# Attention with a cached K and V: K and V requests interleaved, K paced by the transposes, V requested one unit later

## The chip, the cores and the metric

One core of one Trainium2 chip. The metric is the time of one execution in microseconds on the device. All executions that are compared here are of the fast state; two of the repeated executions (404.68 us at a mean clock of 0.992, 400.10 us at 0.996) fell in the slow state and are left out of the ratios. A ratio is the mean time of one kernel's fast runs over the mean of the other kernel's fast runs of the same rounds, so it is not quite the ratio of the medians that are quoted beside it.

## The reference

```python
B, Sq, D = 8, 112, 640
H, Sk, Dh = 32, 512, 192
q = (x @ wq).reshape(B, Sq, H, Dh).transpose(0, 2, 1, 3)
scores = jnp.einsum("bhqd,bhkd->bhqk", q, k_cache) * (Dh ** -0.5)
p = softmax(scores, axis=-1)
o = jnp.einsum("bhqk,bhkd->bhqd", p, v_cache)
return o.transpose(0, 2, 1, 3).reshape(B, Sq, H * Dh) @ wo      # all bf16
```

K and V are 50 MB each and are read once. They are most of the 118.7 MB that the kernel moves.

## The kernel before

The work is cut into 64 units: 8 groups of 4 heads, and 8 batches in each group. K and V of a unit are 0.79 MB each and are requested in four pieces of 192 KB. One engine, SyncE, issues all requests in one list, in order. Each request first waits for its own semaphore values, and while it waits, everything behind it in the list waits too. In the profile of this kernel the list stood so for 39.0 us on K transposes and 29.5 us on PV matmuls.

```python
NK, NV, NT = 3, 4, 3                     # buffers of raw K, of V, of transposed K
...
def load_k(u):
    ...
    for h in range(KP[u]):               # KP[u] is 4
        add(kr[u % NK]..., src[:, cs], mK[u % NK], ...,
            [(vKT, 4 * (u - NK + 1))])   # all four transposes of unit u-3 have ended

def load_v(u):
    for a in range(4):
        add(vs[u % NV]..., v_cache[b, 4 * g + a]..., mV[u % NV], ...,
            [(pPV, u - NV + 1)])         # the PV matmuls of unit u-4 have ended
...
for u in range(4, NU + 1):
    if u < NU:
        load_k(u)
    if u - 1 >= 3:
        load_v(u - 1)
    ...                                  # then this unit's wq or wo pieces, if any
```

What hangs on V and K on the other engines:

```python
# GpSimd: copy three quarters of V into another layout, then (in its own order) reorder wq pieces
def middle(u):
    W(gp, mV[u % NV], 64 * (u // NV + 1))            # all four V pieces of the unit have landed
    W(gp, pPV, u - NM + 1)
    gp.tensor_copy(vm[u % NM]..., vs[u % NV]...).then_inc(gM, 1)

# ScalarE: the last of four exponentials of a unit
def exp(u, a):
    W(act, pS, 4 * u + a + 1)
    if a == 3 and u >= 2:
        W(act, gM, u + 1)                            # the V copy of this unit is done
    ...

# TensorE: scores of a unit
def do_S(u):
    ...
    W(pe, aEX, 4 * u)                                # all exponentials of the unit before
    ...

# TensorE: the first projection of group g waits for all reordered wq pieces
if k == "Q" and c == 0:
    W(pe, gW, DC * g)
```

So a late V reaches TensorE by two ways: V copy, fourth exponential, scores of the next unit; or V copy, wq reordering behind it, first projection of the next group. VectorE transposes K (four instructions for a unit, `do_KT`), and these wait for all four K pieces of the unit.

## Time and profile before

| | before |
|---|---|
| median of the first 3 runs | 392.25 us (391.72 to 393.08) |
| span of the profiled execution | 390.9 us |
| TensorE busy | 385.9 us, 99% |
| DMA engines | 91.6% of the span |
| TensorE idle in the middle of the run | about 1.3 us |

The views are shown in the prediction. In a timeline the columns are start and duration in us, engine, line of the program, operation, output and input tile and the number of merged instructions. What stands in brackets is the engine's idle time just before, and what ended it. A line of the waits view is: waiter, released by; total us, number of times, longest.

### The profile page before, as it was taken

The page shows a single profiled execution, that of the slowest core. Times are in us where ns is not written, and L with a number is a line of the kernel's source. Part 1 is how long each engine was busy: PE and PEld are TensorE (multiplying, and loading weights), DVE is VectorE, ACT ScalarE, POOL GpSimd, SP SyncE. Part 2 cuts the span into 40 slices and gives each one's busy share as a digit, 9 for nine tenths or more (in the row PEclk, how much of TensorE's full clock was granted, in tenths as well). Part 3 has the DMA queues.
Part 4 walks back from the last instruction along what each step waited for, and adds up shares of the span by engine and source line. Part 5 has one row for each costly group of instructions (what it writes and reads, how often), then busy time and mean ns, then how long its engine had stood idle before and what let it go on. Part 6 is the DMA issues. An engine that isn't in the chain of part 4 may idle for free.

```text
span 390.9 us, 19834 instructions
## 1 busy us (share of the span) xinstructions
PE 385.9 (99%) x8865; PEld 243.1 (62%) x8262; DVE 283.3 (72%) x506; ACT 250.3 (64%) x550; POOL 152.7 (39%) x352
## 2 busy tenths in 40 slices
PE   8999989999999999999999999999999999999997
PEld 3555766666666666666665666665666665667764
DVE  1665688687786777776787776876778776789935
ACT  2867765766656765657746667557665667657662
POOL 5442453344343354234352354332553332333331
PEclk9999999999999999999999999999999999999999
DMA  8999999999999999899999999989998789989912
GB/s 266 375 371 373 348 315 368 341 344 366 317 357 338 299 323 351 283 282 313 338 314 319 299 286 350 337 287 294 312 346 289 247 279 296 339 289 303 312 45 70
DMA packets 88585, 120.00 MB, mean 307 GB/s; under 512 B 9777, under 2 KB 88497, under 8 KB 88497
## 3 DMA queue, kind: packets, MB, share of 16 engines
q1 hardware_dynamic: 88496, 118.72, 91.6%
q8 instruction: 68, 1.11, 1.2%
q14 instruction: 21, 0.16, 0.1%
HBM read 117.54 MB, written 1.15 MB: 304 GB/s over the span
## 4 chain that ended last, share of the span: by engine, by line
PE 98%; DMA 1%; DVE 0%; ACT 0%; issue 0%
PE ps L967 22%; PE ps L858 22%; PE ps L928 22%; PE ps L949 21%; PE ps L978 6%; PE ps L887 2%; DMA xs<-in_x_dram 1%; PE ps L854 1%; PE ps L872 1%; PE ps L892 0%; DVE kt L1106 0%; DVE acc L1126 0%; ACT oT L1064 0%; ACT pT L1047 0%; DVE xs L1129 0%
## 5 line engine op out<-in xcount | busy, mean ns | idle before, releaser
L1106 DVE STREAM_TRANSPOSE kt<-kr 128x384 int32<-128x384 int32 x256 | 195.0, 869 | 8.1 <-DMA kr<-in_k_cache_dram 8.1
L1047 ACT ACTIVATE pT<-ps 128x448 bf16<-128x448 f32 x256 | 130.7, 562 | 82.4 <-PE ps L949 82.4
L949 PEld LDWEIGHTS ps<-qT,kt 32*128 32x128 bf16 x6144 | 77.0, 93 | 29.6 <-issue 19.1
L928 PE MATMUL ps<-wos,oT 128*128 128x320 bf16 (+2 forms) x342 | 92.9, 298 | 0.0
L967 PE MATMUL ps<-vm,pT 128*128 128x193 bf16 x768 | 91.5, 247 | 1.1 <-ACT oT L1064 0.8
L858 PE MATMUL ps<-wos,oT 128*128 128x320 bf16 (+1 forms) x340 | 91.3, 296 | 0.0
L1226 POOL TENSOR_SCALAR bad<-rinv 112x4 f32<-112x4 f32 x64 | 14.6, 228 | 195.9 <-DVE rinv L1112 195.9
L949 PE MATMUL ps<-qT,kt 32*128 32x112 bf16 x6144 | 87.3, 208 | 0.4 <-DVE kt L1106 0.3
L967 PEld LDWEIGHTS ps<-vm,pT 128*128 128x128 bf16 x768 | 67.8, 97 | 22.1 <-ACT oT L1064 11.6
L1209 POOL COPY vm<-vs 128x1152 int32<-128x1152 int32 x64 | 73.4, 1147 | 16.9 <-issue 9.5
L858 PE MATMUL ps<-xT,wqs 128*128 128x448 bf16 (+2 forms) x226 | 74.1, 341 | 0.0
L928 PE MATMUL ps<-xT,wqs 128*128 128x448 bf16 (+1 forms) x210 | 73.5, 350 | 0.0
L1054 ACT ACTIVATE os<-ps,rinv 112x192 bf16<-112x192 f32 x128 | 47.9, 436 | 28.5 <-DVE rinv L1112 28.5
L967 PE MATMUL ps<-vs,pT 128*128 128x193 bf16 x256 | 62.6, 245 | 0.0
L928 PEld LDWEIGHTS ps<-wos,oT 128*128 128x128 bf16 x342 | 33.2, 97 | 43.0 <-issue 35.9
L1031 ACT ACTIVATE qT<-ps 128x448 bf16<-128x448 f32 x96 | 47.8, 554 | 18.5 <-PE ps L928 12.6
L1129 DVE TENSOR_TENSOR acc<-ps,acc 128x320 f32<-128x320 f32 x84 | 37.4, 486 | 26.3 <-PE ps L928 26.0
L1064 ACT ACTIVATE oT<-ps 128x672 bf16<-128x672 bf16 x64 | 46.5, 726 | 2.1 <-PE ps L978 2.1
L1112 DVE RECIPROCAL rinv<-ps 112x4 f32<-112x4 f32 x64 | 11.1, 174 | 49.6 <-PE ps L967 49.6
L928 PEld LDWEIGHTS ps<-xT,wqs 128*128 128x128 bf16 x210 | 20.4, 97 | 34.2 <-issue 29.2
L1115 DVE TENSOR_TENSOR os<-ps,rinv 112x384 bf16<-112x384 f32 x64 | 35.7, 558 | 7.3 <-DVE rinv L1112 0.5
L1202 POOL COPY wqs<-wqr 128x384 bf16<-128x384 bf16 x70 | 33.2, 506 | 5.3 <-DMA wqr<-in_wq_dram 5.3
(44 smaller groups left out, 156.3 us busy)
## 6 DMA issues: line engine op xcount, KB each, us to landing
kr<-in_k_cache_dram SPq DMA_DIRECT2D x256, 192.0 KB, 4.2
vs<-in_v_cache_dram SPq DMA_DIRECT2D x256, 192.0 KB, 4.0
wos<-in_wo_dram SPq DMA_DIRECT2D x48, 160.0 KB, 4.2
wqr<-in_wq_dram SPq DMA_DIRECT2D x35, 192.0 KB, 5.3
wqs<-in_wq_dram SPq DMA_DIRECT2D x5, 192.0 KB, 4.3
out_dram<-xs SPq DMA_DIRECT2D x6, 160.0 KB, 1.8
xs<-in_x_dram SPq DMA_DIRECT2D x2, 320.0 KB, 3.4
xs<-in_x_dram SPq DMA_DIRECT2D x1, 480.0 KB, 5.5
```

Of the source, the lines that this page charges most:

```text
L858: return pe.add_instruction(mybir.InstMatmult(name=nc.get_next_instruction_name(), engine=mybir.EngineType.PE, ins=[pe.lower_ap_or_imm(rhs ...
L928: mm = (pe.matmul if h == hs[0] and f == 0 else held)(ps[:, bank_of(pair, h), cs], w, rhs[h][:, cs], q == 0, q == n - 1 and f == cuts - 1)
L949: mm = pe.matmul(ps[:, a, SQ * t:SQ * (t + 1)], kt[u % NT][p, t, c // 2, :, c % 2], qT[g % 2][p, c, SQ * b:SQ * (b + 1)], start=(c == 0), ...
L967: mm = pe.matmul(pv[:, k, e, 0:DH + 1], pT[u % 2][:, a, t, :], src[:, a, v0:v0 + DH + 1], start=(t == 0), stop=(t == 3), skip_group_check= ...
L1031: act.activation(qT[g % 2][:, c, HQ * h:HQ * (h + 1)], ps[:, bank_of_Q0(n) if g == 0 else 6 + h, 0:HQ], ACTF.Copy).then_inc(aQ, 1)
L1047: act.activation(pT[u % 2][:, a, :, 0:SQ], ps[:, a, 0:4 * SQ].rearrange("p (t q) -> p t q", t=4), ACTF.Exp, scale=scale).then_inc(aEX, 1)
L1054: ins = act.activation(os_[u % 2][:, DH * (2 + e):DH * (3 + e)], pv_of(u)[0:SQ, 1, e, 0:DH], ACTF.Copy, scale=rinv[:, u % 4, 2 + e:3 + e])
L1064: act.activation(oT[:, :, SQ * b:SQ * (b + 1)].rearrange("p (k c) q -> p k c q", k=2), src.rearrange("p k (c q) -> p k c q", c=3), ACTF.Co ...
L1106: dve.transpose(dst, src).then_inc(vKT, 1)
L1115: dve.tensor_tensor(os_[u % 2][:, 0:2 * DH].rearrange("p (e d) -> p e d", e=2), pv[0:SQ, 0, :, 0:DH], rinv[:, u % 4, 0:2][:, :, None].broa ...
L1129: ins = dve.tensor_tensor(ob[:, m, cs] if g == NG - 1 else acc[:, m, cs], src, acc[:, m, cs], op=ALU.add)
L1209: gp.tensor_copy(vm[u % NM][:].rearrange("p a (t w) -> p a t w", w=RW)[:, :, :, 0:DH].bitcast(I32), vs[u % NV][:, :, 32:32 + 3 * DH].rearr ...
```

## The change

The intent is to even out the requests. K and V pieces of a unit alternate, each K piece is held until one more transpose has ended, so that requests follow the pace of the consumer, and V is requested with the K of the unit two later in place of one later. One weight piece may go between the second and third pair, another after the fourth.

```diff
-            def load_k(u):
+            def load_k(u, parts=range(4)):
...
-                for h in range(KP[u]):
+                for h in parts:
...
-                        [(vKT, 4 * (u - NK + 1))])
+                        [(vKT, 4 * (u - NK + 1) + (h if u >= 4 else 0))])
-            def load_v(u):
+            def load_v(u, parts=range(4)):
...
-            for u in range(4, NU + 1):
-                if u < NU:
-                    load_k(u)
-                if u - 1 >= 3:
-                    load_v(u - 1)
+            for u in range(4, NU + 2):
+                w = []
...                                       (this unit's wq and wo pieces are put into w)
+                for h in range(4):
+                    if u < NU:
+                        load_k(u, [h])
+                    if u - 2 >= 3:
+                        load_v(u - 2, [h])
+                    if h % 2 and w:
+                        w.pop(0)()
```

More of the change, by code (lines that the diff above doesn't have):

```diff
@@ L1260, in load_wo @@
                         [(pO, 2 * MT * (g - 1))])
-            def load_k(u):
+            def load_k(u, parts=range(4)):
                 g, b = divmod(u, B)
                 src = k_cache[b, 4 * g:4 * g + 4].rearrange("a (j s) d -> (a j) (s d)", s=16)
-                for h in range(KP[u]):
+                for h in parts:
                     cs = slice(16 // KP[u] * DH * h, 16 // KP[u] * DH * (h + 1))
                     add(kr[u % NK][:].rearrange("p s d -> p (s d)")[:, cs], src[:, cs], mK[u % NK], 16 * sum(KP[u % NK:u + 1:NK]),
-                        [(vKT, 4 * (u - NK + 1))])
-            def load_v(u):
+                        [(vKT, 4 * (u - NK + 1) + (h if u >= 4 else 0))])
+            def load_v(u, parts=range(4)):
                 g, b = divmod(u, B)
-                for a in range(4):
+                for a in parts:
                     add(vs[u % NV][:, a, 32:32 + 4 * DH], v_cache[b, 4 * g + a].rearrange("(m t) d -> m (t d)", t=4),
@@ L1298, in on_sync @@
                     if 0 <= d < DC:
-                        load_wq(g, d)
+                        w.append(lambda g=g, d=d: load_wq(g, d))
                 for g in range(1, NG):
@@ L1302, in on_sync @@
                     if 0 <= d < 3:
-                        load_wo(g, d)
+                        w.append(lambda g=g, d=d: load_wo(g, d))
+                for h in range(4):
[5 more added lines that the diff above has]
+                        w.pop(0)()
+                assert not w
             for n, (dst, src, s, count, waits) in enumerate(loads):
```

## The prediction

> **What bounds the kernel now.** I read the page first, then the chain that ended last, then TensorE's own waits, then stretches of time, and only then the timelines of GpSimd, SyncE, ScalarE and TensorE around the places where the DMA queue is full. The page gives the busy times, the DMA row and the chain by engine:
>
> ```profile
> PE 385.9 (99%) x8865; PEld 243.1 (62%) x8262; DVE 283.3 (72%) x506; ACT 250.3 (64%) x550; POOL 152.7 (39%) x352
> ...
> DMA  8999999999999999899999999989998789989912
> ...
> q1 hardware_dynamic: 88496, 118.72, 91.6%
> ...
> PE 98%; DMA 1%; DVE 0%; ACT 0%; issue 0%
> ```
>
> The reader is to see two things near their limit: TensorE has work for 385.9 of 390.9 us, and the DMA engines are taken 91.6% of the time, yet only TensorE is on the chain that sets the end. TensorE's waits are short (columns: waiter, its line, released by; total us, times, longest):
>
> ```profile
> PE ps L984 <- DVE wt L1096: 1.0, 1, 1.0
> PE ps L967 <- ACT oT L1064: 0.8, 1, 0.8
> PE ps L854 <- DMA xs<-in_x_dram: 0.4, 1, 0.4
> PE ps L949 <- DVE kt L1106: 0.3, 1, 0.3
> ```
>
> In the middle of the run TensorE loses only 0.8 + 0.3 us and some 0.2 us more; the rest of its 5.0 us idle lies before the first x piece (some 1.3) and at the end, after all loads (some 2.3). So a perfect supply of K and V can give back about 1.3 us of 392.25, or 0.3%. A loss has no such ceiling: any wait newly put before TensorE stays in the time, since there is almost no slack to recover it.
>
> Where can such a wait come from? The stretches (busy us of PE, PEld, DVE, ACT, POOL; clock; DMA share; GB/s) show where DMA is really short:
>
> ```profile
> 20.00:30.00 10.00, 10.00 (x245) 5.64 (x231) 6.67 (x10) 6.77 (x15) 4.13 (x7) 1.00 1.07 371
> 60.00:70.00 10.00, 10.00 (x257) 6.04 (x238) 8.00 (x14) 5.66 (x13) 4.28 (x10) 1.00 1.06 363
> 200.00:300.00 100.00, 100.00 (x2341) 62.79 (x2158) 75.32 (x134) 63.83 (x143) 40.47 (x90) 1.00 0.97 315
> ```
>
> Up to about 100 us the queue is working off the start-up loads at 350 to 375 GB/s; afterwards demand is near 315. In the first stage V is consumed as soon as it lands. GpSimd's timeline at unit 8 (start, duration, what; in brackets its idle time before), the landing of that unit's V, and the requests on SyncE:
>
> ```profile
> 63.05 1.14 POOL L1209 COPY vm<-vs 128x1152 int32<-128x1152 int32 x1 [2.46 <-issue]
> 64.13 0.95 POOL L1202 COPY wqs<-wqr 128x384 bf16<-128x384 bf16 x2
> ```
>
> ```profile
> L1309 SPq DMA_DIRECT2D vs<-in_v_cache_dram x4: 430/433/439, 56.0 to 57.4; - x4
> ...
> DMA to landing us min/median/max: 4.1/4.3/5.5
> ```
>
> ```profile
> 55.96 1.87 SPq L1309 DMA_DIRECT2D vs<-in_v_cache_dram  x4
> 57.87 0.91 SPq L1309 DMA_DIRECT2D wos<-in_wo_dram  x2
> 58.83 2.30 SPq L1309 DMA_DIRECT2D kr<-in_k_cache_dram  x4
> ```
>
> The last V piece of unit 8 is requested at 57.4 and takes up to 5.5 us: 62.9. GpSimd, idle for 2.46 us, starts its copy of V at 63.05. So what the profile calls "issue" here is a wait for V. The same sum fits units 3 (28.8 + 6.3 = 35.1, copy at 35.28), 4 (34.2 + 5.7, copy at 39.97), 6, 9 and 10: the copy is bound by V's landing from unit 3 to about unit 10. Behind it in GpSimd's order stands the reordering of the last wq piece of the next group, 64.13 to 65.08, and the first projection of that group needs it:
>
> ```profile
> 65.62 0.35 PE L928 MATMUL ps<-xT,wqs 128*128 128x448 bf16 x1
> ```
>
> Slack 0.54 us. This is the thinnest place in the kernel.
>
> [...] So one held K piece holds every request after it, V too. The trace agrees in form: SyncE's waits, 39.0 us for K transposes and 29.5 for PV matmuls, stand between requests. [...] one unit's 96 score matmuls take 1.36 us with DMA at 373 GB/s (at 33 us) and at 84 GB/s (at 372 us). So a smoother DMA does not make matmuls faster. [...] Here no wait exceeds 1.0 us and the clock is 1.000 throughout[...].
>
> **The change part by part.** No bytes, requests, transposes or matmuls are added or removed: 256 K and 256 V requests of 192 KB stay. Three things change.
>
> (a) The hold. Pieces 1 to 3 of K wait for one, two, three more transposes of 0.87 us. The buffer is free already, so this is pacing. In the first stage SyncE arrives late anyway. Unit 9's third hold needs 31 transposes, done at 51.12 + 2.29 = 53.4 us, while its K was requested at 54.06. Cost there about nil. In the later stage the piece goes 3 to 5 us later; six transposes separate the third hold from the first use of that K. I read leads of 7 to 10 us from VectorE's timeline (for example 217.2 to 226.5), against 0.5 us to issue and 4 to 5.5 to land. The thinnest are units 14 and 16 at 5.0 us (81.85 to 86.85), where VectorE may wait some 0.5 us. TensorE has transposes in hand there. Cost 0.
>
> (b) Alternation. SyncE needs 0.46 us for each request, so 9 per unit already take 4.2 of some 5.9 us. The order among them changes, the rate hardly does. Cost 0.
>
> (c) V one unit later. This is the part with a price. V of unit v is complete after the K of unit v+2 instead of before it, and behind one more weight piece. While the queue is backlogged, I count positions. For unit 8 the new end is the old end of unit 10's K, 58.83 + 2.30 = 61.13, plus one wq request, 0.46: 61.6 instead of 57.83, so 3.8 us later. For units 3, 4 and 9 the same count gives 3.9; for 6 and 7 about 5; for 5 about 3.2. (By bytes at 370 GB/s: 0.79 MB of K and 0.39 MB of weights are 3.2 us.)
>
> What takes it up? The fourth exponential of a unit waits for the V copy, the next unit's scores for that exponential. From the copy's end to the exponential, and from its end to the scores, ScalarE's and TensorE's timelines give together 2.1 us for unit 3 (36.43 to 37.25, 37.8 to 39.10), 2.9 for 4, 3.7 for 5, 3.1 for 6, 3.5 for 7, 2.6 for 9, 3.6 for 10. For unit 8 the wq reordering leaves 0.54. Delay less slack: 1.8, 1.0, 0, 2, 1.5, 3.3, 1.3, 0. These do not add up: each microsecond that TensorE has lost gives the next V another microsecond. The largest counts, 3.3 at unit 8. I take off 0.5 because a tail of K waits and queue pressure moves out of the way: 2.8 us in all. After 100 us the copy starts well over 9 us after V's request and nothing is lost. Gains: at most part of the 1.3 us; the 0.8 there is ScalarE's behind a transpose, not DMA's, so none. Sum: 392.25 + 2.8 = 395.0 us.
>
> **The rivals.** First, the smooth supply is neutral: SyncE catches up sooner in the first stage since K stands less in front of waits, V lands only about 2 us later, and the slack takes nearly all of it. For it: the overlap of landing times and the DMA share under 1 at 50 to 60 us. Against it: V is on the edge in six units. It would give 392 to 393. Second, the hold takes the place of the removed burst: VectorE's transposes wait for K in the later stage, and with the in-order queue this feeds back on V. For it: the 5.0 us leads at units 14 and 16. Against it: other leads are 7 us and more, and VectorE is 72% busy. Should it come regularly, 0.2 us in each of 50 units make 402. Third, [...] a few us of half-rate matmuls, 397 to 399. Fourth, a gain over 2%, 7.8 us: there are not that many idle microseconds on TensorE.
>
> **Range and chances.** The mechanism puts it between 1 and 5 us above; the first rival reaches down to 392, the third up to 398 or so. Predicted 395.0, 8 in 10 within 392.2 and 398.2. Faster by over 2%: 0.01. Within 2%: 0.92. Slower by over 2% (above 400.1): 0.07, from the second and third rivals.
>
> **What would show it.** Right: GpSimd's V copies for units 3 to 10 start 3 to 4 us later; TensorE gets waits between 37 and 70 us, the largest for GpSimd's wq reordering, some 3 us, none longer after 100 us; matmul durations and bytes unchanged; K transposes wait under 2 us in all after 80 us. The V hold by position is wrong if V lands less than 2 us later at unit 8. The whole is wrong if TensorE's idle time falls, if its waits are spread over all units, or if score matmuls change their 1.36 us.

That matmuls can run at half rate was measured only afterwards (granted clock 0.50 from 66 to 68 us in the profile of the change). That a held K piece holds V too was also measured afterwards (4.1 us, in hold and V later). For the first stage the profile before has 375 GB/s from 10 to 20 us, 371 to 373 in the 20 us after and 315 to 363 from 40 to 100 us.

## The result, and the profile after

| | before | changed |
|---|---|---|
| median of 6 runs | 392.69 us (391.72 to 393.61) | 399.05 us (397.08 to 400.25) |
| ratio of fast runs | 1 | 1.0159 (95%: 1.0127 to 1.0191) |
| span of the profiled execution | 390.9 us | 396.2 us |

The change makes the kernel slower by 1.6%, or 6.2 us. The prediction had 2.8 us, and its range ended at 398.2. The same fields of the changed kernel's page:

```profile
PE 388.1 (98%) x8865; PEld 244.0 (62%) x8262; DVE 284.0 (72%) x506; ACT 251.5 (63%) x550; POOL 153.3 (39%) x352
...
PEclk9999998999999999999999999999999999999999
DMA  8999999789999999999999989998998979999922
...
q1 hardware_dynamic: 88496, 118.72, 90.5%
...
PE 86%; DMA 4%; issue 4%; SPq 3%; DVE 2%; POOL 1%; ACT 0%; DVEq 0%; ACTq 0%
```

The same bytes and packets are moved. TensorE is busy 2.2 us longer for the same 8865 matmuls, and one slice of the clock row shows an 8. DMA has a hole in the eighth slice, where SyncE now waits for K transposes (6.2 us between 69 and 80 us). The chain that ended last is no longer all TensorE: DMA, SyncE and GpSimd are on it. TensorE's waits:

```profile
PE ps L949 <- ACT pT L1047: 3.2, 3, 2.0
PE ps L984 <- DVE wt L1096: 1.0, 1, 1.0
PE ps L967 <- ACT oT L1064: 0.8, 1, 0.8
PE ps L854 <- DMA xs<-in_x_dram: 0.2, 1, 0.2
```

The first line is new: the scores (L949) wait three times for ScalarE's exponentials. The largest is 2.0 us, before unit 8. It can be followed back through four engines. First SyncE, the last V piece of unit 7, in the kernel before (one burst of four) and in the changed kernel:

```profile
49.99 1.86 SPq L1309 DMA_DIRECT2D vs<-in_v_cache_dram  x4
```

```profile
57.01 0.43 SPq L1314 DMA_DIRECT2D vs<-in_v_cache_dram  x1
```

Then GpSimd's copy of that V, ScalarE's fourth exponential of unit 7 and TensorE's scores of unit 8, first before:

```profile
56.27 1.14 POOL L1209 COPY vm<-vs 128x1152 int32<-128x1152 int32 x1
...
57.78 1.43 ACT L1047 ACTIVATE pT<-ps 128x448 bf16<-128x448 f32 x3
...
61.04 1.36 PE L949 MATMUL ps<-qT,kt 32*128 32x112 bf16 x96
62.33 0.47 PE L978 MATMUL ps<-ident,os 112*128 112x112 bf16 x6
```

and in the changed kernel:

```profile
62.08 1.15 POOL L1209 COPY vm<-vs 128x1152 int32<-128x1152 int32 x1 [4.80 <-issue]
...
63.32 0.54 ACT L1047 ACTIVATE pT<-ps 128x448 bf16<-128x448 f32 x1 [3.64 <-POOL vm L1209]
...
64.01 1.81 PE L949 MATMUL ps<-qT,kt 32*128 32x112 bf16 x96 [1.99 <-ACT pT L1047]
65.75 0.74 PE L978 MATMUL ps<-ident,os 112*128 112x112 bf16 x6
```

The V request ends at 57.44 instead of 51.85, the copy starts 5.8 us later, the exponential waits 3.64 us for it, and TensorE stands for 1.99 us. Then comes something else. The 96 score matmuls take 1.81 us instead of 1.36 and the six transposes 0.74 instead of 0.47: TensorE's clock has dropped, after this wait of 1.99 us and one of 0.83 us some 5 us earlier, and the next stretch of ten microseconds shows it (the last three columns are clock, DMA share, GB/s):

```profile
60.00:70.00 10.00, 8.01 (x145) 4.84 (x131) 4.91 (x10) 3.75 (x8) 4.75 (x9) 0.83 1.03 356
70.00:80.00 10.00, 10.00 (x256) 5.96 (x238) 7.75 (x15) 5.93 (x13) 3.22 (x8) 1.00 0.73 226
```

In steps of 2 us the clock is 0.69 from 64 us, 0.50 from 66, 0.96 from 68 and 1.00 from 70. From the scores of unit 8 to the projection after them TensorE needs 4.58 us before (61.04 to 65.62) and 6.18 us now (64.01 to 70.19): the slow clock costs 1.6 us in this execution. Of the 6 executions 4 had a mean clock of 0.996, and 2 had 1.000.

Where the time goes, unit by unit, I read from VectorE's reciprocal, which starts right after each unit's PV matmuls: its start in one kernel less its start in the kernel before. For the changed kernel the lateness grows by 0.9 us at unit 3, 3.7 at units 7 and 8, 0.4 over units 9 to 17 and 0.3 over the 46 units after (0.1 us came at units 4 to 6). It is mainly the start of the run that is hurt, as predicted; the size is not as predicted.

### The profile page after: what moved, and what is told of

Same layout as the page of the kernel before. It is cut to its first block, busy times and chain, and to the rows that moved or that the text cites. A ratio compares the mean times of both kernels' runs of the same rounds, so it can differ in the third digit from the quotient of the medians.

```text
span 396.2 us, 19834 instructions
## 1 busy us (share of the span) xinstructions
PE 388.1 (98%) x8865; PEld 244.0 (62%) x8262; DVE 284.0 (72%) x506; ACT 251.5 (63%) x550; POOL 153.3 (39%) x352
## 4 chain that ended last, share of the span: by engine, by line
PE 86%; DMA 4%; issue 4%; SPq 3%; DVE 2%; POOL 1%; ACT 0%; DVEq 0%; ACTq 0%
PE ps L967 20%; PE ps L858 19%; PE ps L928 19%; PE ps L949 19%; PE ps L978 6%; DMA kr<-in_k_cache_dram 3%; SPq L1314 3%; PE ps L887 2%; DVE kt L1106 1%; PE ps L854 1%; DMA xs<-in_x_dram 1%; PE ps L872 1%; POOL vm L1209 1%; ACT pT L1047 0%; PE ps L892 0%
## 5 line engine op out<-in xcount | busy, mean ns | idle before, releaser
L1106 DVE STREAM_TRANSPOSE kt<-kr 128x384 int32<-128x384 int32 x256 | 196.1, 872 | 12.4 <-DMA kr<-in_k_cache_dram 12.4
L949 PEld LDWEIGHTS ps<-qT,kt 32*128 32x128 bf16 x6144 | 77.5, 93 | 32.8 <-issue 19.0
L949 PE MATMUL ps<-qT,kt 32*128 32x112 bf16 x6144 | 87.7, 209 | 3.5 <-ACT pT L1047 3.2
```

The lines of the kernel that those rows point to most:

```text
L949: mm = pe.matmul(ps[:, a, SQ * t:SQ * (t + 1)], kt[u % NT][p, t, c // 2, :, c % 2], qT[g % 2][p, c, SQ * b:SQ * (b + 1)], start=(c == 0), ...
L1106: dve.transpose(dst, src).then_inc(vKT, 1)
```

## The experiments

All were run with 5 rounds and all gave correct results. The median of the kernel before was between 392.71 and 393.31 us in each call, so 0.1% is 0.4 us. The four calls ran on four different chips, so kernels of one call compare more safely than kernels of two. In the rows with alternation a weight piece goes out after the second and the fourth pair, as in the change; only the row "weights last" puts them behind all V pieces.

| kernel | hold | alternation | V later | ratio to before (95%) | median us |
|---|---|---|---|---|---|
| changed, again | yes | yes | yes | 1.0167 (1.0142 to 1.0193) | 399.14 |
| V later only | | | yes | 1.0077 (1.0058 to 1.0097) | 395.45 |
| V later only, again | | | yes | 1.0051 (1.0028 to 1.0073) | 395.36 |
| hold only | yes | | | 1.0006 (0.9985 to 1.0027) | 393.21 |
| alternation only | | yes | | 1.0215 (1.0191 to 1.0238) | 401.45 |
| alternation and hold | yes | yes | | 1.0232 (1.0201 to 1.0263) | 402.82 |
| alternation and V later | | yes | yes | 1.0120 (1.0098 to 1.0143) | 397.56 |
| the same, weights last | | yes | yes | 1.0081 (1.0060 to 1.0101) | 396.22 |
| hold and V later | yes | | yes | 1.0121 (1.0088 to 1.0153) | 397.10 |

**First call: the parts one by one.** My theory A was the prediction's: V later is what costs, in the start-up backlog, with the clock added. The rival B was the hold.

The changed kernel again, for a second profile:

> The changed kernel once more, for its spread and a second profile. Theory A (V one unit later starves the V copy in the first 70 us, TensorE stands before the scores of unit 8, and its clock drops there): 397 to 400 us, 4 to 5 us of the loss by unit 8, a stretch of lowered clock between 60 and 70 us in most executions. Theory B (the hold on K pieces is what costs): the same time, so this run tells nothing between them.

399.14 us, and in its profile the clock stayed at 1.000: a span of 395.2 us with 3.9 us of waits before scores. Two of these three waits are in the first stage, the third comes after it:

```profile
100.40 1.36 PE L949 MATMUL ps<-qT,kt 32*128 32x112 bf16 x96 [1.06 <-ACT pT L1047]
```

Five of its 6 executions were fast, two of them at 0.996. Over both measurements the 5 fast executions at 1.000 have a mean of 398.0 us and the 6 at 0.996 one of 399.6 us.

V one unit later only, K in bursts without a hold:

```diff
                 if u < NU:
                     load_k(u)
-                if u - 1 >= 3:
-                    load_v(u - 1)
+                if u - 2 >= 3 and u - 2 < NU:
+                    load_v(u - 2)
```

> K pieces in bursts without a hold, only V requested one unit later. Theory A: nearly the whole loss, 396 to 400 us, with V copies of units 3 to 8 some 4 to 6 us later than before. Theory B (hold): near 393 us.

395.45 us, 0.8% or 3.0 us. That is close to the prediction's own figure for this part, 2.8 us, and half of the change's loss. A second measurement, in the fourth call, gave 2.0 us, a third of it. The waits of TensorE show both ways by which V was to reach it, the exponential and, at the predicted place, the wq reordering:

```profile
PE ps L949 <- ACT pT L1047: 1.6, 2, 1.0
PE ps L984 <- DVE wt L1096: 1.0, 1, 1.0
PE ps L928 <- POOL wqs L1202: 0.9, 1, 0.9
```

Theory A said nearly the whole loss; it got half.

The hold only, in the order of the kernel before:

```diff
-                        [(vKT, 4 * (u - NK + 1))])
+                        [(vKT, 4 * (u - NK + 1) + (h if u >= 4 else 0))])
```

> The order and bursts of the kernel before, each K piece held for one more transpose. Theory A: 392 to 393.5 us, since the queue arrives later than the hold in the first stage. Theory B: 396 us or more, with VectorE waiting for K.

393.21 us, no difference. Rival B falls in its plain form: the hold alone costs nothing in the mean. Its profiled execution shows something else. TensorE had two short waits around the scores of unit 7, and after them its clock was lowered from about 58 to 62 us (mean clock of this execution 0.996), which shows in the PV matmuls (0.56 us for three):

```profile
56.41 0.57 PE L949 MATMUL ps<-qT,kt 32*128 32x112 bf16 x31 [0.96 <-issue]
58.21 0.56 PE L967 MATMUL ps<-vm,pT 128*128 128x193 bf16 x3 [0.82 <-ACT oT L1064]
```

At the same place in the kernel before, with the second wait only, they take 0.43 us:

```profile
57.95 0.43 PE L967 MATMUL ps<-vm,pT 128*128 128x193 bf16 x3 [0.85 <-ACT oT L1064]
```

Alternation only, with V where it was and no hold:

```diff
+                for h in range(4):
+                    if u < NU:
+                        load_k(u, [h])
+                    if u - 1 >= 3 and u - 1 < NU:
+                        load_v(u - 1, [h])
+                    if h % 2 and w:
+                        w.pop(0)()
```

> K and V pieces alternately, V of the unit before as in the kernel before, no hold. Theory A: 392 to 393.5 us. A third theory, that the interleaving itself slows the landing of both, since the last of four pieces comes later: V copies 1 to 2 us later at units 3 to 8, 393.5 to 395 us. Theory B: as before.

401.45 us, worse than the whole change. None of the three theories had this. V is in time now (unit 7 copied at 57.61, before 56.27, of which 1.2 us are a later start of this execution), and up to unit 9 the kernel loses nothing. But VectorE waits for K all through the run; in the kernel before this was 8.1 us in 4 times:

```profile
DVE kt L1106 <- DMA kr<-in_k_cache_dram: 52.1, 37, 3.7
```

SyncE's timeline in the later stage shows why:

```profile
210.49 0.44 SPq L1314 DMA_DIRECT2D kr<-in_k_cache_dram  x1
212.69 0.33 SPq L1314 DMA_DIRECT2D vs<-in_v_cache_dram  x1
213.06 0.43 SPq L1314 DMA_DIRECT2D kr<-in_k_cache_dram  x1
```

After the first K piece of a unit the next in the list is a V piece that must wait for a PV (210.93 to 212.69). The other three K pieces stand behind it, although their buffer is free. In the kernel before all four K pieces were out before that wait.

**Second call: pairs, and the stage.** Theory C, formed on the first call: once V is late, the hold on a K piece also delays the V piece behind it. Theory D: V later is what makes alternation bearable.

Alternation and V later, without the hold (the changed kernel's loop, the hold's term taken out):

> K and V pieces alternately and V one unit later, no hold; with the hold missing from the change. If the hold costs nothing once V is late (theory A, as in the prediction): as the changed kernel, near 399 us. If the hold on a K piece delays the V piece behind it in the same queue after about 65 us (theory C, formed on the first four runs): 396 to 397.5 us, with V copies of units 10 to 16 some 2 us earlier than in the changed kernel.

397.56 us, 1.2%. It is as theory C has it, between V later alone and the whole change. Its interval still overlaps a little with those of the changed kernel. Its V copies of units 10 to 16 start 1.5 to 3.5 us earlier than in the changed kernel, of which 1.3 to 2.2 us are because this execution as a whole is ahead there.

Hold and V later, in bursts:

> K pieces in bursts, held, and V one unit later. Theory A: as V later alone, 395.5 us. Theory C: 396.5 to 398.5 us, the loss by unit 9 as with V later alone (2.5 to 3 us) and some 1 us more between units 10 and 16.

397.10 us, 1.2%, again as theory C. SyncE's timeline shows the hold at work. The K pieces of unit 14 and the V pieces of unit 12 behind them, first in V later alone, then with the hold:

```profile
80.22 1.85 SPq L1309 DMA_DIRECT2D kr<-in_k_cache_dram  x4
82.12 1.85 SPq L1309 DMA_DIRECT2D vs<-in_v_cache_dram  x4
```

```profile
81.76 4.41 SPq L1309 DMA_DIRECT2D kr<-in_k_cache_dram  x4
86.22 1.86 SPq L1309 DMA_DIRECT2D vs<-in_v_cache_dram  x4
```

The four K requests take 4.41 us in place of 1.85, and V goes out 4.1 us later; only 0.6 us of this is a later state of the whole execution. The profiles of all kernels with V later separate cleanly after the first stage. Lateness gained over units 9 to 17, by the reciprocals: with the hold 0.4 and 1.1 us (changed, two profiles) and 0.4 (this one); without it -0.4 in this call's alternating kernel and -0.4 in V later alone. Two later profiles with the hold gave 0.9 and 1.0, two without it -0.4 each. So five profiles with the hold lie 0.8 to 1.5 us above four without. (The -0.4 is the zero line: the hold alone gives it too, so it is the one profile of the kernel before that lost 0.4 us there.) ScalarE waited for a V copy 9 or 10 times in the changed kernel and this one, 5 to 7 times in the two without.

Alternation and hold, V in its old place:

> Alternately and held, V of the unit before (not later). The run with alternation alone showed VectorE waiting 52 us for K, since K pieces stand behind V pieces that wait for a PV. Theory D: that is a crossing of two waits in one queue, the hold makes it no better, 400 to 406 us, and V one unit later is what makes alternation bearable. If the hold evens it out instead: 393 to 397 us.

402.82 us, and VectorE waits 51.2 us for K: theory D. The hold does not help alternation; V later does, by taking the PV wait out of K's way. With alternation it saves 3.7 us (1.0215 to 1.0120), with alternation and hold 2.7 (1.0232 to the 1.0163 of the changed kernel's two measurements), even though it costs 2 to 3 us by itself.

The whole change from unit 24 on only, the old order before:

```diff
+                late = u >= 24
...                                       (late: the changed loop; else: the loop of before)
+                        [(vKT, 4 * (u - NK + 1) + (h if u >= 24 else 0))])
```

> The order of the kernel before up to unit 23, the whole change from unit 24 on. All theories that put the loss into the start-up backlog (A, C): 392 to 393.5 us. If the change costs a little in every unit: 395 us or more.

393.08 us, ratio 1.0009 (0.9989 to 1.0030). The change costs nothing where the queue has no backlog, and gains nothing there either.

**Third call: the wait itself, and the queue position.** Here the kernel before was made to wait at unit 8 with all its loads as they were:

```diff
                 W(pe, aEX, 4 * u)
+                if u == 8:
+                    W(pe, vKT, 38)        # 39 in the second kernel
```

> The kernel before; TensorE alone is held before the scores of unit 8 until two more K transposes have ended, so that it stands there some 2.3 us, with all loads as before. If a wait costs only its own length: +2.3 us, 395 us. If the clock drops after it as in the profile of the changed kernel (some 4 us at a lower rate): +3.5 to +4.5 us, 396.5 to 397 us, in some or all executions, with a mean clock of 0.996 in those.

396.57 us, ratio 1.0072 (1.0037 to 1.0108). The executions fall into two kinds: 394.55 and 394.98 us at a mean clock of 1.000, and four from 396.49 to 398.02 at 0.996. In the profiled one the wait grew to 4.2 us, because K came late for that transpose, so the length of the wait is less well known than I had wanted.

> The same with one more transpose, a wait of some 3.1 us. Own length only: +3.1 us, 395.8 us. With the clock's drop: +4.5 to +6 us, 397.5 to 399 us. [...]

397.61 us, ratio 1.0104 (1.0074 to 1.0134). The wait was 3.07 us as set:

```profile
63.50 2.43 PE L951 MATMUL ps<-qT,kt 32*128 32x112 bf16 x96 [3.07 <-DVE kt L1108]
65.86 0.74 PE L980 MATMUL ps<-ident,os 112*128 112x112 bf16 x6
```

One execution kept 1.000 and took 396.1 us; the five others had 0.991 or 0.996 and took 397.36 to 398.25. From the scores to the next projection it is 7.47 us (63.50 to 70.97) in place of 4.58: the slow clock cost 2.9 us there, almost as much as the wait.

The changed kernel with the three wo loads of group 1 three units later:

```diff
-                    d = u - (8 * g - 1)
+                    d = u - (8 * g - 1) - (3 if g == 1 else 0)
```

> The changed kernel, but the three wo loads of group 1 requested with units 10 to 12 in place of 7 to 9. If the V of unit 7 is late because of what stands before it in the queue: its copy 1.5 to 2 us earlier than in the changed kernel, the wait before the scores of unit 8 under 1 us, the clock stays up, 396 to 397.5 us; units 10 to 13 may lose up to 1 us more. If the position in the queue is not it: 399 us.

397.08 us, ratio 1.0105 (1.0073 to 1.0137), about 2.3 us less than the changed kernel. The total is as expected, the way only in part: V of unit 7 was copied at 61.40, just 0.7 us earlier than in the changed kernel. TensorE's waits moved to units 3 and 7 (it gained 1.8 us of lateness at unit 3 and 0.8 over units 4 to 6) and only 0.4 us came at units 7 and 8, without a drop of the clock in the profiled execution. One profile can't say how much is position and how much is the clock.

The kernel before with V ahead of K up to unit 13:

```diff
+                if u < 14:
+                    load_v(u - 1)
                 if u < NU:
                     load_k(u)
-                if u - 1 >= 3:
+                if u >= 14:
                     load_v(u - 1)
```

> The kernel before with V ahead of K in each unit up to 13. V copies of units 3 to 10 some 2 us earlier. Since no wait of TensorE in the kernel before comes from V: 392 to 393.5 us, the same. If V on the edge costs the kernel before something that its one profile does not show: up to 1 us less. If K then comes late: 394 us or more.

393.68 us, ratio 1.0019 (0.9981 to 1.0057): the same. V copies at units 3 and 8 came 2.2 and 1.7 us earlier, at unit 9 1.3 us, at units 4 to 7 only 0.4 to 1.2 us, and from unit 10 on not at all. V on the edge costs the kernel before nothing that this could take away.

**Fourth call: what was still open.** V later alone had explained half. Left were the clock, and what alternation and hold add.

The changed kernel with TensorE kept at work before unit 8, by matmuls of zeros into a bank that the scores then overwrite:

```diff
+                if u == 8:
+                    W(pe, aEX, 4 * u - 3)
+                    for j in range(36):   # 56 in the next kernel
+                        (held if j else pe.matmul)(ps[:, 0, 0:112], wt[:], wt[:, 0:112], True, True)
                 W(pe, aEX, 4 * u)
```

> The changed kernel, with 36 matmuls of zeros (some 1.7 us at the full clock) before the wait for the scores of unit 8, into a bank that is then overwritten. If the lowered clock after that wait is part of the loss (theory E): no or shorter stretches of lowered clock near unit 8, and 0.5 to 2 us less than the changed kernel in the mean, 397 to 398.5 us. If the drop costs nothing of note or stays: 399 us or more.

The 1.7 us of this expectation is an estimate that the profile before bears out: its projection matmuls of 320 columns start 0.136 us apart, so 112 columns are 0.048 us, 36 of them 1.7 us and 56 of them 2.7.

398.89 us, ratio 1.0156 (1.0128 to 1.0184), so not clearly less than the changed kernel. The clock was 1.000 in 5 of 6 executions, as intended, but the work of zeros takes 1.9 us whether or not there is a wait to fill, and executions at 1.000 still ranged from 396.95 to 400.11. This is inconclusive on the size. The changed kernel's loss is not mainly the clock: its own executions at 1.000 have a mean of 398.0 us, some 5 us above the kernel before.

> The kernel before with the wait of some 3.1 us before the scores of unit 8, filled with 56 matmuls of zeros (some 2.7 us). Theory E: only the wait's own length is left, +3 us, 396 us, clock 1.000. Otherwise as without the filling, 397.6 us.

396.50 us, ratio 1.0088 (1.0068 to 1.0108). All six executions had 1.000, and the scores after the filled wait take their usual time:

```profile
64.57 1.36 PE L955 MATMUL ps<-qT,kt 32*128 32x112 bf16 x96 [0.35 <-DVE kt L1112]
```

Beside 2.43 us and one execution of six at 1.000 in the unfilled twin, this shows that here the idleness before the scores brings the drop. What that is worth in the mean is less clear: 1.1 us by the medians, 0.6 by the ratios, and the intervals overlap.

Alternation and V later, no hold (its term taken out as before), with weight pieces after V:

```diff
-                    if h % 2 and w:
-                        w.pop(0)()
-                assert not w
+                for f in w:
+                    f()
```

> Alternately and V one unit later, no hold, but each unit's weight pieces after its V pieces as in the kernel before. If the weight piece ahead of the last V pieces is what alternation adds over V later alone: 395.5 to 396.3 us, last V requests of units 4 to 9 as with V later alone. If it is the alternation of K and V itself: near 397.5 us.

396.22 us, ratio 1.0081 (1.0060 to 1.0101), against 1.0120 (1.0098 to 1.0143) with the weight piece in front of the last two V pieces. The last V requests of units 4 to 9 go out 0 to 1.8 us earlier than with the weight piece in front and within 2 us of those of the first profile of V later alone, so the expectation holds roughly. The weight piece is thus probably most of what alternation added to V later, some 1.5 us; but the two were measured in different calls, and their intervals just touch. The profiled execution here was a late one, 398.45 us, and it shows the predicted wait of the first projection for the wq reordering at full size:

```profile
PE ps L928 <- POOL wqs L1202: 2.2, 1, 2.2
```

V later alone, again:

> V one unit later alone, again, beside the alternating kernel on the same chip: 395.5 us, +0.8%. If it comes out near 397 us, the difference between it and the kernels with alternation or hold added was one of chip and call, and only the whole change against V later alone is clear.

395.36 us, ratio 1.0051 (1.0028 to 1.0073). Its profiled execution, the slowest of the fast ones, waits 3.9 us before scores, 2.04 of it before unit 8, and only 0.3 us for the wq reordering. The scores after that wait of 2.04 us took their 1.36 us, and the mean clock of this execution was 1.000: a wait of this length was not always followed by a lowered clock. Its interval and that of the alternating kernel with weights last overlap a little, so whether alternation costs anything beyond the weight piece stays open. Against both kernels with a further part added to V later (1.012), this measurement of V later alone is clearly less; the first one (1.0077, up to 1.0097) is below the alternating kernel too, but its interval overlaps with that of hold and V later (from 1.0088).

No version beat the kernel before, and none was indicated by the runs: TensorE has only some 1.3 us of idle time in the middle.

## Why the prediction was wrong, point by point

**The bound and the ceiling on a gain: right.** TensorE remained the bound, no kernel was faster, and in the profiles shown a unit's 96 score matmuls took 1.36 us where the clock was up.

**Part (c), V later: right in mechanism and in total, taken alone; the place was wrong.** The V copies of units 3 to 6 start 2.7, 2.9, 3.5 and 3.8 us later, and unit 8's 3.6 us (predicted 3 to 4, with 3.8 for unit 8). The part by itself costs 3.0 and 2.0 us in two measurements, and 2.8 was predicted. That total is in part luck. It was to come from the wq reordering at unit 8, but in the two profiles of V later alone this wait is 0.9 and 0.3 us, and the waits for exponentials make 1.6 and 3.9. In the profile of the change the place was off by one unit. I took unit 7's delay as about 5 us and its slack as 3.5, which makes 1.5. The 3.5 was misread: the fourth exponential starts at 58.67, 1.26 us after the copy's end, and ends 1.83 before the scores, together 3.1 (for unit 5 it is 3.3, not 3.7). The copy was 5.8 us late. The slack, as the changed kernel used it, was smaller still: from the copy's end at 57.41 to the scores at 61.04 are 3.63 us, of which the exponential and its hand-over need 0.78 (63.23 to 64.01 in the changed kernel), so 2.85. The difference is the 3.0 us by which the scores of unit 8 came late. After that, and after the slow clock, unit 8's own wait was covered: the reordering ended at 68.70, and the projection started at 70.19. In the kernel with weights last unit 7 passed more lightly, and the predicted wait appeared, 2.2 us.

**Part (a), the hold: this step failed.** "Cost 0" holds for the hold alone, 1.0006. It does not hold with V late: in bursts the ratio with it is 1.0121 against 1.0077 and 1.0051, which is 1.7 and 2.8 us (1.1 and 1.3 if medians are compared), and with alternation 1.0159 and 1.0167 against 1.0120, 1.5 and 1.9 us: some 2 us. I had looked for the hold's cost at VectorE, as a K that comes late. K waits did grow, from 8.1 us to 12.4, and about 4 us of the 12.4 lie after 80 us where I had allowed 2. But the path to TensorE was the other one: a held K piece holds the V pieces behind it, which had lost their reserve. The prediction itself says that a held K piece holds V too, and then costs the hold as if V stood elsewhere. "After 100 us the copy starts well over 9 us after V's request and nothing is lost" failed with it: in four of the five profiles with the hold TensorE still waits, up to 1.06 us, between 94 and 117 us. Over units 9 to 17 all five lose 0.8 to 1.5 us more than those without. The rest of the 2 us is not placed.

**Part (b), alternation: this step failed too.** "The order among them changes, the rate hardly does" misses that order is what decides whose wait stands in front of whom. With V in its old place alternation alone costs 8.4 us. With V later most of that goes, and what is left is probably mainly the weight piece that now stands in front of the last two V pieces: I had counted one such piece in (c), for unit 8, as 0.46 us, but it seems to cost some 1.5 us in all.

**The rivals.** The first (neutral) fell. The second was right that hold and in-order queue feed back on V, and wrong about the stage and about VectorE as the place where it shows. The third, a lowered clock, was given little weight, with nothing in a trace to go by, and came in 6 of 11 fast executions of the changed kernel, after a wait of only 2.0 us in the profiled one; executions with it are 1.6 us longer in the mean, so if the drop is what makes them longer, it adds about 0.9 us to the mean. The parts (2 to 3 for V, some 2 for the hold, some 1.5 for the weight piece) come to 5.5 to 6.5 us, against 6.2 and 6.6 measured; the clock is contained in them. The agreement is a weak test: V later alone, then alternation, weight piece and hold added one by one end at the changed kernel whatever the parts are, so only the hold, found in two pairs, is checked by it. They come from differences between kernels, not from one trace, and the profiled executions, which lose 4.3 to 5.3 us, do not show all of it. Why executions of the changed kernel differ by 2 us at the same clock is open.

## What to carry to other kernels

In one in-order request list, cost a change by whose wait stands before whose request, and cost its parts together: here a hold that was free while the next stream had reserve (1.0006) was not free when the same change took the reserve away (some 2 us). Look for the consumer that starts the moment its data lands (here V's copy, in the start-up backlog); there places lost in the list were delays (V copies 2.7 to 3.8 us later at units 3 to 6), whereas the same order from unit 24 on cost nothing (1.0009). Where TensorE is the bound, a wait can cost more than its length: here the lowered clock after 3.07 us of waiting took another 2.9 us.
